# A fused two-attention kernel: the list that orders all of its work is replaced by another list

## The chip, the core and the metric

The kernel runs on one core of one Trainium2 chip. The core has five engines with queues of their own, filled when the program is built: TensorE (PE in the profile; its weight loads are shown as PEld), VectorE (DVE), ScalarE (ACT), GpSimd (POOL) and SyncE (SP). Every engine takes its instructions strictly in the order of its queue and waits, where needed, on semaphores of the others. The metric is the device time of one execution in microseconds (us); lower is better.

## The reference, cut to what matters

Two attentions over 2048 tokens of width 640 (32 heads of 20) are computed and laid side by side in a bf16 output of 2048 x 1280.

```python
# A: four segments of 512 tokens, with a memory carried from one to the next
for s in range(4):
    logits = einsum('bhqd,bhkd->bhqk', qs, ks) * scale + mask      # causal within the segment
    a_dot  = einsum('bhqk,bhkd->bhqd', softmax(logits), vs)
    pq     = phi(qs)                                               # phi(t) = t+1 if t>0 else exp(t)
    a_mem  = einsum('bhld,bhde->bhle', pq, M) / (einsum('bhld,bhd->bhl', pq, z) + 1e-6)
    o      = g * a_mem + (1 - g) * a_dot                           # g = sigmoid(beta)
    M      = M + einsum('bhld,bhle->bhde', phi(ks), vs);  z = z + phi(ks).sum(l)
out_A = o @ wo                                                     # q, k, v = x @ wq, wk, wv
# B: sliding window
mask   = (i - j >= 0) & (i - j < 256)
out_B  = (softmax(where(mask, q @ k.T * scale, -1e9)) @ v) @ wo    # q, k, v = x @ wqkv
```

## The kernel before

**Chunks and jobs.** The work is cut into eight chunks of 512 tokens, A and B in turn: chunk 0 is A's first segment, chunk 1 is B's first 512 tokens, up to chunk 7, B's last. Each chunk has generators ("jobs") that issue one piece of work at a time. Their names are letter, chunk, part: `k70` is the first part of the k projection of chunk 7. The letters are `q`, `k` and `v` (projections; `qk_job`, `v_job`), `d` (the update of A's memory), `o` (output projection, two halves of 320 columns for each of four tiles of 128 tokens; `final_job`) and `z0`, `z1` (the last two tiles of chunk 7, which are transposed on TensorE instead of by a DMA; `last_job`). A piece is one wide product of 128 rows, five of them to a tile of 320 or 512 columns.

**Score batches.** There are 153 batches of scores, `S` or `s` in the list (`score_batch`). A batch is a run of small products of 20 rows, `sc<-qA,kA` or `sc<-qB,kB` (L818), into two PSUM tiles; ScalarE then takes two exponentials of 128x1024 (L834) into `pt`. There are three PSUM score tiles of two banks (`NSC`) and ten `pt` (`NPT`). Masks are applied to `pt` by GpSimd (affine select, L873) or VectorE (L851).

**Value and memory products.** `A` in the list is the value product of one group of four heads (`av`, L887) or, in chunk 7, of one tile (`av_tile`, L908); `M` is the product with A's memory (`mem`, L934 or L939). VectorE turns the result (L953), then the row sum is inverted (L972, L978, L981) and GpSimd normalises (L991); where both a value and a memory product exist they are added by VectorE (L1004).

**Two banks.** Every wide product tile, value product and memory product accumulates in one of two PSUM banks (`m0`, `m1`). It can begin when the one before in that bank has been emptied: by the turn (L953) after `A` and `M`, by a cast (L557 for k and q, L734 and L739 for v, L1095 on VectorE or L1078 on ScalarE for o) after a projection tile.

**Forms.** Scores and value products use TensorE in tiles of 32 rows or columns. A wide product can be run whole (128x128 weights, L939) or as four products of 32 output columns (L934). The form is fixed per stretch between two score batches: where the list has `S` followed by an `A` before the next batch, the wide products of that stretch are issued in four; after `s` they are issued whole.

**Transfers.** q and k tiles are regrouped by a round trip to memory (L509, L517); so are the squares of v at the diagonals (L757, L783) and the feature maps of k (L651 out, L646 back, turned). The normalised `o` of a chunk goes out to `scr_o` (L1025) and comes back turned as `oT` or `xT` (DMA_TRANSPOSE, L1044), after which the `o` jobs can run. Weights come in by L319 and L331, x by L355. Most of these are in SyncE's queue.

**The order.** `body` builds the program with a model of the engines' clocks (class `Flow`). The string `PLAN` is the order of TensorE's work: the main loop pops its next entry and issues it as soon as its needs are met in that model, so TensorE's queue follows the list exactly. Instructions of the other engines (casts, masks, turns, norms, transfers) are put into their queues at the times that the model gives, so their order follows the list indirectly. `X*n` stands for n entries of X. "Slot n" is the stretch between batch n and batch n+1; batch 0 is the first.

## Time and profile before

| | |
|---|---|
| median of 3 runs | 330.41 us (329.88 to 330.71) |
| profiled execution | 330.69 us, of which 329.0 us is the span |
| granted TensorE clock | 1.00 |
| TensorE busy | 314.1 us (95%), 7180 matmuls |
| ScalarE busy | 299.8 us (91%), 334 instructions |
| GpSimd busy | 266.2 us (81%), 674 |
| VectorE busy | 257.7 us (78%), 534 |
| exponentials (L834) | 282.9 us, 306 of 1024 ns on average |
| masks on GpSimd (L873) | 178.7 us, 512 |
| turns (L953) | 61.3 us, 88 |
| score products (L818) | 39.9 + 33.4 us in the two largest groups |
| DMA | 47.12 MB in 75017 packets, mean 143 GB/s |

The span is the time from the first to the last instruction in the trace, the rest is around it. A row of a timeline is: start (us), duration, engine, line, operation, output <- inputs with sizes, how many instructions the row holds, and in brackets the idle time of the engine before it and what released it. In a row with several instructions the duration is that of the whole row. A row of the waits is: who waited, on what, the sum in us, how many times, and the longest.

### The profile page before, as it was taken

The page shows a single profiled execution, that of the slowest core. Times are in us where ns is not written, and L with a number is a line of the kernel's source. Part 1 is how long each engine was busy: PE and PEld are TensorE (multiplying, and loading weights), DVE is VectorE, ACT ScalarE, POOL GpSimd, SP SyncE. Part 2 cuts the span into 40 slices and gives each one's busy share as a digit, 9 for nine tenths or more (in the row PEclk, how much of TensorE's full clock was granted, in tenths as well). Part 3 has the DMA queues.
Part 4 walks back from the last instruction along what each step waited for, and adds up shares of the span by engine and source line. Part 5 has one row for each costly group of instructions (what it writes and reads, how often), then busy time and mean ns, then how long its engine had stood idle before and what let it go on. Part 6 is the DMA issues. An engine that isn't in the chain of part 4 may idle for free.

```text
span 329.0 us, 16969 instructions
## 1 busy us (share of the span) xinstructions
PE 314.1 (95%) x7180; PEld 177.2 (54%) x7215; DVE 257.7 (78%) x534; ACT 299.8 (91%) x334; POOL 266.2 (81%) x674
## 2 busy tenths in 40 slices
PE   8999999999999999999899999999999999999994
PEld 3454546555544455556554546456654445666662
DVE  6777757799877877999777897988777788976672
ACT  2979999999999998989899999899999999979972
POOL 8466689988769799977785999999975899989760
PEclk9999999999999999999999999999999999999999
DMA  7975846753679565265688146018758027398522
GB/s 206 400 249 142 186 140 115 162 168 70 166 190 190 106 166 166 44 137 148 126 223 176 30 86 181 20 36 171 143 175 179 14 53 183 110 234 164 115 95 67
DMA packets 75017, 47.12 MB, mean 143 GB/s; under 512 B 47133, under 2 KB 71933, under 8 KB 74941
## 3 DMA queue, kind: packets, MB, share of 16 engines
q1 hardware_dynamic: 74221, 45.38, 57.2%
q8 instruction: 56, 0.92, 1.1%
q10 hardware_dynamic: 720, 0.66, 0.7%
q14 instruction: 20, 0.16, 0.1%
HBM read 17.62 MB, written 16.79 MB: 105 GB/s over the span
## 4 chain that ended last, share of the span: by engine, by line
PE 48%; POOL 9%; ACT 7%; DVE 5%; issue 4%; POOLq 0%; ACTq 0%; DVEq 0%
PE m L939 25%; PE sc L818 10%; PE m L887 7%; ACT pt L834 6%; POOL pt L873 6%; PE m L934 5%; DVE tt L953 3%; POOL o L991 2%; PE m L908 1%; POOL u L991 1%; DVE pt L851 1%; PE m L686 0%; POOL rr L972 0%; ACT e L577 0%; POOL MZ L710 0%
## 5 line engine op out<-in xcount | busy, mean ns | idle before, releaser
L834 ACT ACTIVATE pt<-sc 128x1024 bf16<-128x1024 f32 (+2 forms) x306 | 282.9, 1024 | 14.0 <-PE sc L818 12.1
L873 POOL TENSOR_SCALAR_AFFINE_SELECT pt<-pt 128x128 bf16<-128x128 bf16 (+1 forms) x512 | 178.7, 377 | 47.9 <-ACT pt L834 40.4
L953 DVE STREAM_TRANSPOSE tt<-m 128x512 f32<-128x512 f32 x88 | 61.3, 709 | 24.7 <-PE m L887 16.8
L991 POOL TENSOR_TENSOR o<-tt,rr 128x320 bf16<-128x320 f32 x64 | 48.5, 759 | 3.6 <-DVE rr L981 2.6
L818 PE MATMUL sc<-qB,kB 20*64 20x64 bf16 (+2 forms) x1728 | 39.9, 217 | 0.8 <-ACT pt L834 0.5
L851 DVE TENSOR_TENSOR pt<-pt,ends 128x1024 bf16<-128x1024 bf16 (+2 forms) x50 | 36.5, 739 | 0.0
L939 PEld LDWEIGHTS <-xT 128*128 128x128 bf16 x286 | 25.8, 97 | 17.7 <-issue 6.8
L1095 DVE CAST ot<-m 128x320 bf16<-128x320 f32 x58 | 27.9, 486 | 8.3 <-PE m L939 7.0
L818 PEld LDWEIGHTS <-kB 20*64 20x64 bf16 (+1 forms) x1728 | 22.2, 98 | 22.6 <-issue 20.6
L818 PE MATMUL sc<-qA,kA 20*64 20x64 bf16 (+4 forms) x1024 | 33.4, 237 | 0.5 <-ACT pt L834 0.3
L939 PEld LDWEIGHTS <-oT 128*128 128x128 bf16 x244 | 21.6, 97 | 11.3 <-issue 1.6
L818 PEld LDWEIGHTS <-kA 20*128 20x128 bf16 (+1 forms) x1024 | 13.6, 97 | 22.8 <-issue 21.8
L939 PE MATMUL m<-wBv,xT 128*128 128x320 bf16 x147 | 24.2, 299 | 1.0 <-DVE tt L953 0.4
L887 PE MATMUL m<-pt,vA 128*32 128x192 bf16 (+3 forms) x512 | 23.6, 274 | 0.2
L939 PE MATMUL m<-xT,wBq 128*128 128x512 bf16 x73 | 20.6, 380 | 0.9 <-DVE tt L953 0.3
L939 PE MATMUL m<-wo_A,oT 128*128 128x320 bf16 x125 | 20.4, 300 | 0.3 <-DVE kA L557 0.3
L939 PE MATMUL m<-wv_A,xT 128*128 128x320 bf16 x119 | 20.0, 300 | 0.6 <-DVE qA L557 0.5
L939 PE MATMUL m<-xT,wBk 128*128 128x512 bf16 x70 | 19.6, 380 | 0.7 <-issue 0.3
L739 DVE CAST vB<-m 128x320 bf16<-128x320 f32 x32 | 15.6, 486 | 4.7 <-PE m L939 2.4
L557 DVE CAST kB<-m 128x512 bf16<-128x512 f32 x20 | 13.6, 680 | 6.7 <-PE m L939 5.7
L557 DVE CAST qB<-m 128x512 bf16<-128x512 f32 x20 | 13.8, 688 | 6.5 <-PE m L934 3.2
L939 PE MATMUL m<-wo_B,oT 128*128 128x320 bf16 x109 | 18.7, 300 | 0.2 <-DVE ot L1095 0.2
(127 smaller groups left out, 468.8 us busy)
## 6 DMA issues: line engine op xcount, KB each, us to landing
out_dram<-ot SPq DMA_DIRECT2D x29, 160.0 KB
scr_o<-o SPq DMA_DIRECT2D x28, 160.0 KB
xT<-in_B_x_dram SPq DMA_DIRECT2D x8, 288.0 KB
xT<-in_A_x_dram SPq DMA_DIRECT2D x8, 256.0 KB
scr_pk<-e SPq DMA_DIRECT2D x15, 128.0 KB
vS<-vA SPq DMA_DIRECT2D x16, 87.0 KB
vL<-vB SPq DMA_DIRECT2D x8, 174.0 KB
scr_kA<-kA SPq DMA_DIRECT2D x16, 60.0 KB
```

What stands on the lines that cost most here:

```text
L557: nc.vector.tensor_copy(out=dst[:, m, at:at + L], in_=ps[:, :])
L739: nc.vector.tensor_copy(out=dst, in_=src)
L818: nc.tensor.matmul(ps[j // 2][h0:h1, j % 2, c0:c0 + nq], lhsT=k[rows, g, k0:k0 + h1 - h0], rhs=q[rows, g, q0:q0 + nq], start=True, stop=Tr ...
L834: nc.scalar.activation(out=pt[:, :, lo:hi], in_=ps[i][:, :, lo:hi], func=ACT.Exp, scale=self.scale)
L851: nc.vector.tensor_tensor(out=blk, in0=blk, in1=self.ends[:, c0, :].unsqueeze(1).unsqueeze(1) .to_broadcast([P, 2, n // SH, SH]), op=ALU.mult)
L873: nc.gpsimd.affine_select(out=blk, in_=blk, pattern=pat, compare_op=ALU.is_ge, fill=self.zero, base=base, channel_multiplier=mul)
L887: nc.tensor.matmul(O[HD * j:HD * j + HD, q0:q0 + nq], lhsT=v[:, at:at + HD], rhs=pts[j // 2][:, j % 2, c0:c0 + nq], start=(n_ == 0), stop= ...
L934: self.nc.tensor.matmul(ps[s, 0:n], lhsT=lhsT[:, s], rhs=rhs, start=start, stop=stop, tile_position=(0, HD * j), skip_group_check=True)
L939: self.nc.tensor.matmul(ps[:, 0:n], lhsT=lhsT, rhs=rhs, start=start, stop=stop, skip_group_check=True)
L953: self.nc.vector.transpose(out=tt[:], in_=O[:, :])
L991: nc.gpsimd.tensor_tensor(out=to[:] if add_to else to, in0=a, in1=b, op=ALU.mult)
L1095: nc.vector.tensor_copy(out=ot[:, 320 * hf:320 * hf + 320], in_=ps[:, 0:320])
```

## The change

Only the string `PLAN` differs. Both lists hold every entry the same number of times, apart from the two letters of the score batches: `S` goes from 77 to 83 and `s` from 76 to 70. 114 of the 154 stretches (before the first batch, between batches, after the last) hold other work than before. The jobs, the buffers, the model and the transfers themselves are the same code.

```diff
-    "k00*5 q00*5 k01*4 S k01 q01*5 S v00*16 S v00*4 k02 S k02*4 k03*5 q02*3 S q02*2 q03*5 k04*5 "
-    "A S A q04*5 v01 s v01*9 s k10*5 S v01*10 S q10*2 A S q10*3 q11*3 S q11*2 q12*5 A s k11*5 "
-    "k12*2 S k12 A k12*2 S v10*9 S v10*10 S v10 A k13*2 s k13*3 q13*4 S q13 A s k14*5 q14*2 S "
-    "q14*2 A q14 S d2*5 v11*4 S v11*8 S v11*3 A v11 S v11*4 d2*2 S q20*4 A s q20*5 s q20*6 "
-    "k20*6 S k20*4 A s k20*5 v20*5 S v20*3 A v20 s v20 q23*5 v20 s v20*8 S v20 q23*5 A s v21*5 "
-    "k23*3 S k23*2 A s o00*5 k23*5 v21*5 S o00*5 v21*5 S A v21*5 s q30*5 k30*2 S k30*3 A s "
-    "k30*6 S k30*4 q30 S q30*4 A s M q30*5 v30*2 s v30*3 A S M v30*10 s A M s v30*5 q33*4 S q33 "
-    "A s M k33*5 q33 s q33*4 k33*3 S k33*2 A s M v31*8 S v31*2 A M S v31*10 S A M S d4*5 q40*3 "
-    "S q40*2 d4*2 A s M k40*5 s q40*10 S v40*5 k40*5 A S k40*5 v40*5 S v40*2 A v40*2 S v40*6 "
-    "q43*3 S q43*7 S k43*10 A S o00*5 A s o10*10 s o00*5 o10*5 S o00*10 v41*4 S v41 o10*5 A "
-    "o00*2 s o00*3 v41*5 S A o00*5 s v41*8 s v41*2 o10*7 S o10*3 A o10*3 s o10*2 q50*5 S A "
-    "k50*3 s k50*2 k53*5 s q50*5 k50*2 s k50*3 A S k50*2 M k50*3 s A M S v50*5 q50*5 s A M S "
-    "v50*10 S v50*5 A s M q53*6 s q53*4 k53*2 S k53*3 A S M v51*9 S v51 A M S v51*10 S A M S "
-    "q60*5 d6*5 s d6*2 A S k60*2 M k60*3 q60*5 s k60*6 S k60*4 q60*5 A S q63*5 v60*5 S A v60*5 "
-    "s q63*5 v60*2 S v60*3 k63*5 S v60*5 A k63 S k63*4 o10*5 S o20*3 A s o20*7 s v61*10 S v61*5 "
-    "A v61*5 S o30*5 o20*5 S o20*5 A o20 S o20*4 o30*4 s o30 o20*10 S A o20*4 S o20 k70*7 S k70 "
-    "A k70*2 S k70*5 v70*3 S v70*2 q70*4 s q70 A M s q70*5 s A q70*5 s v70*5 k73*2 s k73*3 A s "
-    "M v70*9 s v70 A M s q73*2 M q73*3 s k73*5 q73*2 s q73*3 A s o30*5 M s v71*5 A s M v71*5 "
-    "o30*4 s o30 A M s v71*8 s v71*2 A M s o30*9 s o30 o40*5 o30*5 s o30*5 A s o40*10 s o40*15 "
-    "A s o40*5 o50*5 s o40*5 o50*5 s A o50*4 s o50*6 s A o50*4 s o50*8 s o50*8 s A o60*5 s "
-    "o60*10 o70*5 s A o70*3 s o70*2 o60*7 s o60*8 o71*2 s o71*3 o60*2 A o60*3 z0 o71*5 o60 A "
-    "o60 z0 o60*3 z0 z1*2 z0 z1*2 ")
+    "k00*5 q00*5 k01*4 S k01 q01*5 v00*2 s v00*14 S v00*4 k02*5 S q02*5 q03*3 S q03*2 k03*5 "
+    "k04*5 A S A q04*5 v01 S v01*9 s v01*5 k10 S k10*4 v01*5 S q10*2 A S q10*3 q11*3 S q11*2 "
+    "k11*5 A S q12*5 k12*2 S k12 A k12*2 S v10*7 s v10*12 S v10 A k13*2 s k13*3 k14*4 S k14 A S "
+    "q13*5 q14*2 S q14 A q14*2 s d2*5 v11*2 S v11*10 S v11*3 A v11 S v11*4 d2*2 S k20 A k20*3 S "
+    "k20 q20*4 s q20*11 k20 S k20*4 A s k20*5 v20*5 S v20*4 A s v20 q23*6 s q23*4 v20*4 S v20 "
+    "v21*5 A S v20*5 k23*3 S A k23*2 S o00*5 k23*5 v21*4 S v21 o00*5 v21*6 S v21*4 A s q30*5 "
+    "k30*2 S k30*3 A S q30*6 S q30*4 k30*2 S k30*3 A S M v30*5 k30*2 s A k30*3 s M q33*5 v30 s "
+    "v30*4 A s M v30*8 S A v30*2 s k33*2 M k33*3 S v31*5 q33*2 S q33*3 A S k33*2 M k33*3 v31*3 "
+    "S v31*2 A M s v31*10 S A M s d4*5 q40*3 S q40*2 d4*2 A S M k40*5 q40*3 S q40*7 S v40*5 "
+    "k40*5 A S k40*5 v40*5 S v40 A v40*3 S v40*6 q43*3 S q43*7 S k43*10 A S o10*5 A s o10*5 "
+    "o00*5 s o00*10 o10*5 S v41*5 o00*4 S o00 v41*5 A v41 S v41*4 o00*5 S A o00*5 S o10*5 v41*5 "
+    "s o10*9 S o10 A o10*3 S o10*2 k53*5 S A k50*4 s k50*6 s q50*7 s q50*3 A S k50*2 M k50*3 S "
+    "A M s v50*5 q50*5 s A M s v50*10 S v50*5 A S M q53*6 S q53*4 k53*2 S k53*3 A S M v51*10 s "
+    "A M s v51*9 S v51 A M s d6*5 q60*5 S d6*2 A S k60 M k60*6 S k60*3 q60*5 S q60*5 k60*5 A S "
+    "q63*5 v60*5 S A v60*4 S v60 q63*5 k63*3 s k63*2 o10*5 S v60*5 A v60*2 s v60*3 k63*5 S "
+    "o20*3 A S o20*2 v61*6 s v61*4 o20*5 o30 S o30*4 A v61*5 s o30*5 v61*5 S o20*5 A S o20*9 s "
+    "o20*9 S o20*2 A o20*4 s o20 k70*5 S A v70*5 s q70*5 k70 S k70*4 q70*2 s q70*3 A s q70*2 M "
+    "q70*3 s k70*5 A s v70*5 k73*2 s k73*3 A s M v70*10 s A M s q73*2 M q73*3 s q73*5 k73 s "
+    "k73*4 A s o40*5 M s o30*5 A s M o40*5 o30*3 s o30*2 A M s v71*5 o30*3 s o30*2 A M s o30*5 "
+    "v71*4 s v71*10 s v71 A o30*4 s o30 o40*5 o30*2 s o30*3 o40*15 A s o40*9 s o40 o50*7 s "
+    "o50*3 A o50 s o50*9 s A o50*2 s o50*9 s o50*9 s A o60*5 s o70*5 o60*5 s o60*5 A o60*3 s "
+    "o60*2 o70*5 o71*2 s o71*3 o60*5 s o60*5 A o60*5 z0 o71*5 A z0 o60*2 z0 o60*3 z1*2 z0 z1*2 ")
```

Some places in the lists, slot by slot:

| slot | before | after |
|---|---|---|
| 36, 37, 38 | `o00*5 k23*5 v21*5`, `o00*5 v21*5`, `A v21*5` | `o00*5 k23*5 v21*4`, `v21 o00*5 v21*6`, `v21*4 A` |
| 59, 60 | `M k40*5`, `q40*10` | `M k40*5 q40*3`, `q40*7` |
| 129, 130, 131 | `o30*5 M`, `v71*5 A`, `M v71*5 o30*4` | `o40*5 M`, `o30*5 A`, `M o40*5 o30*3` |
| 134, 135, 136 | `v71*2 A M`, `o30*9`, `o30 o40*5 o30*5` | `o30*2 A M`, `o30*5 v71*4`, `v71*10` |
| 137, 138, 139 | `o30*5 A`, `o40*10`, `o40*15 A` | `v71 A o30*4`, `o30 o40*5 o30*2`, `o30*3 o40*15 A` |
| 148, 149 | `o60*10 o70*5`, `A o70*3` | `o70*5 o60*5`, `o60*5 A o60*3` |
| 150, 151 | `o70*2 o60*7`, `o60*8 o71*2` | `o60*2 o70*5 o71*2`, `o71*3 o60*5` |

## The prediction

> **What bounds the kernel now.** I read the page first (busy shares, the chain that ended last), then the waits, then the busy time by stretches, then timelines at single places. "Slot n" is the work the list puts between score batch n and score batch n+1 (153 batches, 0 to 152).
>
> ```profile
> span 329.0 us, 16969 instructions
> PE 314.1 (95%) x7180; PEld 177.2 (54%) x7215; DVE 257.7 (78%) x534; ACT 299.8 (91%) x334; POOL 266.2 (81%) x674
> q8 instruction: 56, 0.92, 1.1%
> PE 48%; POOL 9%; ACT 7%; DVE 5%; issue 4%; POOLq 0%; ACTq 0%; DVEq 0%
> ```
>
> ```profile
> POOL pt L873 <- ACT pt L834: 40.4, 57, 2.1
> ACT pt L834 <- PE sc L818: 12.1, 22, 1.8
> PE m L939 <- DVE tt L953: 1.3, 6, 0.3
> PE m L887 <- issue: 0.8, 1, 0.8
> PE sc L818 <- ACT pt L834: 0.8, 4, 0.3
> ```
>
> ```profile
> core 0: us, PE busy (x) PEld busy (x) DVE busy (x) ACT busy (x) POOL busy (x), PEclk, DMA share, GB/s
> 8.20:46.30 38.10, 37.32 (x713) 19.24 (x717) 27.81 (x59) 35.38 (x42) 23.75 (x70) 1.00 0.75 221
> 46.30:79.50 33.20, 32.24 (x796) 18.28 (x785) 26.80 (x54) 32.35 (x39) 31.14 (x71) 1.00 0.60 146
> 187.50:219.70 32.20, 31.15 (x723) 16.95 (x716) 27.88 (x57) 29.80 (x33) 31.12 (x74) 1.00 0.32 76
> 255.00:299.70 44.70, 43.85 (x997) 25.14 (x997) 36.80 (x79) 42.67 (x46) 40.70 (x106) 1.00 0.52 118
> ```
>
> TensorE (PE) is busy 95% of the span and ScalarE (ACT) 91%; in every stretch of the middle both are within a few per cent of full, at the granted clock of 1.00. Neither alone is the bound: ScalarE has run dry 22 times waiting for scores (12.1 us in all), and TensorE has waited for score buffers that the exponentials had not freed (0.8 us by this view, which sees only the part beyond modelled ends). So the end is set by a path that changes sides: it runs along TensorE up to a place where ScalarE ran dry, and along ScalarE up to a place where TensorE waited for it. An order can win in two ways: score batches placed so that ScalarE stays fed, and fewer waits in the stretches where TensorE carries the path.
>
> **TensorE's own work.** The order listing of the two built programs counts 192 groups of four 32-column matmuls for the wide products before and 193 after (360+408 and 396+376 instructions), 881 and 880 whole matmuls, 340 and 339 changes between array shapes; every score, value and memory product is there as often as before.
>
> ```profile
> 236.41 0.86 PE L934 MATMUL m<-wo_A,oT 128*32 128x320 bf16 x20
> 237.10 0.28 PE L887 MATMUL m<-pt,vX 128*32 128x256 bf16 x4
> ...
> 309.27 0.84 PE L939 MATMUL m<-wo_B,xT 128*128 128x320 bf16 x5
> 310.05 0.40 PE L818 MATMUL sc<-qB,kB 20*128 20x128 bf16 x16
> ```
>
> Five products of 320 columns take 0.69 us in four-column form up to a value product of the same shape (236.41 to 237.10), and 0.78 us whole up to a score, where the array shape changes (309.27 to 310.05): 0.136 a piece either way and 0.1 for the change. One change fewer is 0.1 us; the exchange of forms is nothing, and there is no cover to lose, since this is TensorE's own time. **Term 1: -0.1** (ends -0.1 and 0).
>
> **Where the score batches stand.** I laid the lists side by side and priced each slot by such spacings. 114 of 154 stretches hold other work, but the distance of a batch from the start of the list changes by at most 0.9 us (batch 3) and stands 0.2 us earlier at batch 152. Both lists are variants of one layout. What counts is the places where ScalarE had run dry.
>
> ```profile
> 130.34 1.02 ACT L834 ACTIVATE pt<-sc 128x1024 bf16<-128x1024 f32 x1 [0.66 <-PE sc L818]
> 293.20 3.79 ACT L834 ACTIVATE pt<-sc 128x1024 bf16<-128x1024 f32 x4 [1.78 <-PE sc L818]
> 310.56 7.48 ACT L834 ACTIVATE pt<-sc 128x1024 bf16<-128x1024 f32 x8 [0.44 <-PE sc L818]
> ```
>
> Slot 59 gains three pieces of q40 and slot 60 loses them: batch 60 comes 0.65 later, batch 61 at its old place. ScalarE, which needs 2.04 for a batch (7.48 for eight exponentials shows the rate), then finishes batch 60 0.1 after the moment at which it now starts batch 61: +0.1. Slots 140 to 148 put batch 149 0.68 earlier, so its wait of 0.44 goes; but slot 149 grows from 1.61 to 2.38 us of TensorE work, batch 150 stands 0.09 later in the list than before, and about 0.05 of the gain is left at the last exponential. The long wait before batch 140 (1.78) grows with slot 139 (eighteen products of 320 where there were fifteen) while slots 135 to 138 give as much back. The others move by 0.1 to 0.4, up and down, and return within some slots. **Term 2: 0** (ends -0.6, the 0.44 and 0.1 to 0.2 more kept, and +0.4, the largest lateness that a dry place gets, if it stays).
>
> **Waits for the two accumulator banks.** Every wide product, value product and memory product takes one of two banks and waits for VectorE (DVE) to empty the one before it.
>
> ```profile
> 259.87 0.59 PE L887 MATMUL m<-pt,vA 128*32 128x448 bf16 x12
> ...
> 260.54 0.48 PE L818 MATMUL sc<-qA,kA 20*128 20x448 bf16 x8
> 260.95 0.39 PE L939 MATMUL m<-pq,MZ 128*128 128x512 bf16 x1
> 261.48 1.38 PE L939 MATMUL m<-wBv,xT 128*128 128x320 bf16 x9
> ```
>
> Here a value product, a score batch and one memory product (M) are followed by a product that needs the value product's bank: 0.53 us from M to the next start where 0.216 is M's spacing, so 0.31 lost, with 0.68 us of other work since the value product's last piece. Where 0.68 covers, 0.16 to 0.39 are lost in this trace; at 0.78 about 0.2; from 0.89 on next to nothing. After a value or output tile (a shorter evacuation) a cover of 0.81 loses about 0.07. Counting covers in both lists: below 0.8 us after a value or memory product 19 before, 15 after; output and v tiles at 0.81 and under 26 before, 32 after; two q/k tiles come down to 0.86 and 1.04 us where some 1.17 is wanted. Priced alike, the sum of what is lacking is 9.4 before and 9.5 us after, and of that the part in the stretches where TensorE carries the path grows by 0.24. **Term 3: +0.25** (ends -0.5, if only the four removed shortest covers count, and +0.6, if all new ones do).
>
> ```profile
> 82.97 0.34 PE L818 MATMUL sc<-qB,kB 20*128 20x256 bf16 x8
> 83.60 0.84 PE L939 MATMUL m<-wo_A,oT 128*128 128x320 bf16 x5 [0.29 <-DVE kA L557]
> 84.61 0.84 PE L939 MATMUL m<-wv_A,xT 128*128 128x320 bf16 x5 [0.17 <-DVE vA L734]
> ```
>
> ```profile
> 82.50 0.45 DVE L598 TENSOR_TENSOR e<-r,e 128x512 bf16<-128x512 bf16 x1
> 82.87 0.68 DVE L557 CAST kA<-m 128x512 bf16<-128x512 f32 x1
> 83.47 0.68 DVE L851 TENSOR_TENSOR pt<-pt,ends 128x1024 bf16<-128x1024 bf16 x1
> 84.07 0.48 DVE L734 TENSOR_TENSOR vA<-m,omg 128x320 bf16<-128x320 f32 x1
> ```
>
> Slot 37 is of another kind: there the cover is long enough, but VectorE is behind. The k tile's cast stands behind the feature map of an earlier k tile (0.42 + 0.45), and the v tile's behind a mask of 0.68. Batch 37 takes 0.33 to the next start elsewhere, so the output product starts 0.3 late, and the v product another 0.33 late (84.61 less 83.60 less 0.68). In the new order the cast stands ahead of that feature map, between the two masks, and the output product comes one piece later. This stretch feeds a place where ScalarE ran dry. I take two thirds of the 0.65 as gone: **term 4: -0.45** (ends -0.65 and 0). What is late next is the fourth v tile, which now begins ahead of batch 38.
>
> **Code loading.** In slot 73 the weight loads stop in the middle of a value product, and nothing the profile shows ended the stop:
>
> ```profile
> 159.25 0.10 PEld L887 LDWEIGHTS <-vL 128*32 128x32 bf16 x3
> 160.30 0.09 PEld L887 LDWEIGHTS <-vL 128*32 128x32 bf16 x1 [0.95 <-issue]
> ```
>
> The instruction queue moved 0.92 MB in 56 pieces, one for each 256 or so of TensorE's instructions, and this stop is the only one near 1 us. The new list has the same number of instructions ahead of slot 73 and 3.51 us of work for the 256 before the stop (3.48 before). **Term 5: 0** (ends -0.95, the stop gone, and +0.95, a second one). The Trainium skill, Runtime: NRT & Kernel Launch, section Instruction fetch mechanics, says that the sequencer streams blocks of 256 instructions ahead and that this is hidden by the slower issue; the 0.95 us speak against it at this place, and by the rule alone the stop would be no matter of the order and the sum would keep the same terms without it.
>
> **Loads and queues.** SyncE's queue is emptied in order. In the new list the last chunk's transposed tiles are wanted earlier:
>
> ```profile
> 286.44 2.58 SPq L1044 DMA_TRANSPOSE oT<-scr_o  x1
> 302.46 1.22 SPq L1044 DMA_TRANSPOSE xT<-scr_o  x1
> 310.09 1.21 SPq L1044 DMA_TRANSPOSE xT<-scr_o  x1
> ```
>
> The first product of tile 1 (o71) moves from slot 151 into slot 150 behind seven products. Batch 150 stands some 1.6 us behind batch 149 (310.05), takes 0.65, and seven products 0.95: 313.3, 2.0 us after the issue at 310.09 has ended. The first use of tile 0 before was at 309.27, 5.6 us after its issue ended (302.46 + 1.22), and does not wait; it moves to the front of slot 148, 1.4 us earlier. The transpose at 286.44 waits for a buffer that o30 frees; o30 ends in slot 139 instead of 137, some 2.6 us later, and scr_o6 and all behind it on SyncE start later by what the queue's pauses do not absorb. Loads of the last output weights, on the other hand, leave SyncE before the last regrouping instead of within it, and o10, o30 and o40 begin earlier in slots where their tiles have long been stored. **Term 6: 0** (ends 0 and +1.9: the 5.6 are the only proven landing, and 3.7 of them may be needed where 2.0 are left, rounded up for the queue). GpSimd and VectorE keep their counts (674 and 534); ScalarE's list moves by three feature-map steps.
>
> **The tail** from the last exponential on has the same steps in both lists; the last value product stands 0.14 us later on TensorE, behind masks that were just ready, and what TensorE last waits for is the last normalised tile (o):
>
> ```profile
> 321.90 0.40 PE L1118 MATMUL sc<-one,o 128*128 128x128 bf16 x4 [0.33 <-POOL o L991]
> ```
>
> **Term 7: 0** (ends 0 and +0.14).
>
> **Sum.** -0.1 + 0 + 0.25 - 0.45 + 0 + 0 + 0 = -0.3 us. The profiled execution took 330.69 us (329.0 of span and 1.7 around it), 0.28 above the median 330.41 of the runs: 330.4 against its own time, 330.1 against the median. I give 330.3. About 0.3% (1 us) is what a measurement of this kernel can tell from no change.
>
> **Rivals.** *Late transposed tiles (slower).* If o71 and o70 wait for SyncE, the wait stands right ahead of the last two score batches and goes through to the end: term 6 at its upper end, 330.3 + 1.9 = 332.2. It decides when tile 1 needs over 2.0 us from the end of its issue to use, or when the queue is 0.5 to 1 us later than now. For it: three things now hang on o30's end. Against it: the pauses in SyncE's queue. Chance 0.15. *Bank waits at the new places (slower).* More covers at 0.81 and the VectorE order at new places cost like slot 37 cost before: two such places at 0.65 on top of the sum, 331.6. Chance 0.17. *The stop goes (faster).* The block that came late in slot 73 comes in time: 330.3 - 0.95 = 329.35. For it: the stop came once in 56 blocks. Against: equal counts ahead of it. Chance 0.14. *ScalarE stays fed (faster).* Terms 2 and 3 at their lower ends: 330.3 - 0.6 - 0.75 = 328.95. Chance 0.18. *The order does nothing to speak of* is the forecast itself: 0.36, from 329.5 to 331.3.
>
> The range reaches from a little below the last faster case to a little above the slower one: 328.5 to 332.6. Faster by over 0.3%: 0.14 + 0.18 = 0.32; within: 0.36; slower: 0.15 + 0.17 = 0.32.
>
> **What would show it.** Right: TensorE busy within 0.5 us of 314.1; ScalarE's waits for scores still between 11 and 13 us; no wait of kA or vA casts in slot 37; the stop of about 0.95 in slot 73 again; no product of L939 waiting for a DMA after 300 us. Wrong: a second stop without a releaser, a product waiting for xT or oT, or waits for scores that change by over 1 us in the last 50 us.

## The result and the profile after

The kernel with the new list takes 333.91 us (333.64 to 336.02), the one before 330.47 us in the same comparison. The ratio is 1.0121 with a 95% interval of 1.0078 to 1.0164: slower by 1.2%, beyond the upper end of the range that was given (332.6). The profiled execution took 333.64 us with a span of 331.9. An execution that took over 1.5% longer than the fastest of the same kernel is left out of the medians and ratios below; there are two such (335.16 and 342.15 us).

The page of the profile after, its lines on the span, the engines and the chain that ended last:

```profile
span 331.9 us, 16976 instructions
PE 314.8 (95%) x7182; PEld 176.5 (53%) x7218; DVE 258.0 (78%) x534; ACT 300.3 (90%) x334; POOL 265.6 (80%) x674
...
PE 45%; POOL 12%; DVE 10%; ACT 4%; issue 3%; DMA 3%; SPq 1%; POOLq 0%; ACTq 0%; DVEq 0%
```

The engines do as much as before; the loss is in waiting. The chain has a new entry, DMA with 3%, and VectorE's part doubled from 5% to 10%. The waits of the profile after (who waited for what, sum in us, how often, longest) name transfers for which TensorE waited; the profile before has no wait of TensorE for xT or oT out of scr_o:

```profile
ACT pt L834 <- PE sc L818: 12.4, 24, 1.9
...
PE m L939 <- DVE tt L953: 1.6, 7, 0.3
...
PEld L939 <- DMA xT<-scr_o: 1.2, 1, 1.2
...
PEld L939 <- DMA oT<-scr_o: 0.7, 1, 0.7
...
PE m L887 <- DVE vB L739: 0.7, 1, 0.7
```

Where the time was lost is read from the exponentials: the start of a batch's first exponential in the trace after, less the same in the trace before.

| batch | 49 | 54 | 73 | 74 | 100 | 121 | 144 | 145 | 149 | 150 | 151 |
|---|---|---|---|---|---|---|---|---|---|---|---|
| after less before, us | 0.0 | 2.0 | 2.0 | 1.0 | 1.0 | 0.7 | 0.7 | 1.4 | 1.4 | 2.2 | 3.1 |

Two places lose (batches 50 to 54, and from batch 145 on), one gains (slot 73). ScalarE's timeline at the first place before, and after at the two places, with idle times in brackets:

```profile
103.06 22.37 ACT L834 ACTIVATE pt<-sc 128x1024 bf16<-128x1024 f32 x24
```

```profile
109.25 5.61 ACT L834 ACTIVATE pt<-sc 128x1024 bf16<-128x1024 f32 x6 [0.61 <-PE sc L818]
115.34 1.94 ACT L834 ACTIVATE pt<-sc 128x1024 bf16<-128x1024 f32 x2 [0.49 <-PE sc L818]
118.10 7.45 ACT L834 ACTIVATE pt<-sc 128x1024 bf16<-128x1024 f32 x8 [0.82 <-POOL rr L972]
...
304.04 5.61 ACT L834 ACTIVATE pt<-sc 128x1024 bf16<-128x1024 f32 x6 [0.56 <-PE sc L818]
310.15 3.77 ACT L834 ACTIVATE pt<-sc 128x1024 bf16<-128x1024 f32 x4 [0.51 <-POOL pt L873]
314.62 1.94 ACT L834 ACTIVATE pt<-sc 128x1024 bf16<-128x1024 f32 x2 [0.69 <-PE sc L818]
317.36 3.77 ACT L834 ACTIVATE pt<-sc 128x1024 bf16<-128x1024 f32 x4 [0.80 <-PE sc L818]
```

Before, ScalarE went through batches 47 to 58 without a pause (the 24 exponentials of the first row). Three things stand ahead of the pauses after. The first is on VectorE (TensorE's rows below it):

```profile
111.26 0.68 DVE L851 TENSOR_TENSOR pt<-pt,ends 128x1024 bf16<-128x1024 bf16 x1
113.42 0.49 DVE L739 CAST vB<-m 128x320 bf16<-128x320 f32 x1 [1.48 <-PE m L934]
113.83 0.68 DVE L851 TENSOR_TENSOR pt<-pt,ends 128x1024 bf16<-128x1024 bf16 x1
```

```profile
110.88 0.85 PE L939 MATMUL m<-wBv,xT 128*128 128x320 bf16 x5
111.57 0.59 PE L939 MATMUL m<-xT,wBq 128*128 128x512 bf16 x2
...
112.48 0.83 PE L934 MATMUL m<-xT,wBq 128*32 128x512 bf16 x12
```

The cast of v31's first tile (`vB`) waits 1.48 us. The product that it empties is the first of these rows and had ended near 111.7; the L934 that the cast's row names is a product of q, which the cast does not read and which ended just before it. The second is in SyncE's queue and what waits for it (SyncE's second transpose before, which the prediction does not show, then SyncE after, then TensorE after):

```profile
297.36 3.81 SPq L1044 DMA_TRANSPOSE oT<-scr_o  x1
```

```profile
290.58 2.76 SPq L1044 DMA_TRANSPOSE oT<-scr_o  x1
...
302.90 2.50 SPq L1044 DMA_TRANSPOSE oT<-scr_o  x1
305.58 1.86 SPq L1044 DMA_TRANSPOSE xT<-scr_o  x1
...
312.03 1.21 SPq L1044 DMA_TRANSPOSE xT<-scr_o  x1
```

```profile
113.97 0.59 PE L887 MATMUL m<-pt,vA 128*32 128x448 bf16 x12 [0.66 <-DVE vB L739]
...
308.85 0.85 PE L939 MATMUL m<-wo_A,oT 128*128 128x320 bf16 x5 [0.61 <-DMA oT<-scr_o]
...
316.46 0.45 PE L939 MATMUL m<-wo_B,xT 128*128 128x320 bf16 x2 [0.84 <-DMA xT<-scr_o]
```

The four transposes are issued 4.1, 5.5, 3.1 and 1.9 us later than before, and o60 (slot 147) and o71 (slot 150) wait for theirs; measured from start to start, TensorE loses 0.68 and 1.00 us. The third is the loading of code. TensorE's weight loads after, at two of the stops:

```profile
108.99 0.11 PEld L818 LDWEIGHTS <-kA 20*64 20x64 bf16 x4 [0.68 <-issue]
...
303.43 0.45 PEld L818 LDWEIGHTS <-kB 20*64 20x64 bf16 x46 [0.66 <-issue]
```

Counted in TensorE's queue, these stops lie where a block of 256 instructions ends (every 256 from the 194th on, waits on semaphores counted), as does the one of slot 73 before. After, there are four: 0.79 us in slot 50, 0.48 in slot 69, 0.32 in slot 98 and 0.74 in slot 145, measured from start to start beyond the usual spacing. The one in slot 73 is gone.

### The profile page after: what moved, and what is told of

It is laid out like the page before. It is cut to its first block, busy times and chain, and to the rows that moved or that the text cites. A ratio compares the mean times of both kernels' runs of the same rounds, so it can differ in the third digit from the quotient of the medians.

```text
span 331.9 us, 16976 instructions
## 1 busy us (share of the span) xinstructions
PE 314.8 (95%) x7182; PEld 176.5 (53%) x7218; DVE 258.0 (78%) x534; ACT 300.3 (90%) x334; POOL 265.6 (80%) x674
## 4 chain that ended last, share of the span: by engine, by line
PE 45%; POOL 12%; DVE 10%; ACT 4%; issue 3%; DMA 3%; SPq 1%; POOLq 0%; ACTq 0%; DVEq 0%
PE m L939 22%; PE sc L818 9%; POOL pt L873 7%; PE m L887 7%; PE m L934 5%; ACT pt L834 4%; DVE tt L953 4%; POOL o L991 2%; DVE pt L851 1%; DMA xT<-scr_o 1%; DMA vU<-vB 1%; PE m L908 1%; POOL u L991 1%; DVE ot L1095 1%; DVE vA L734 1%
## 5 line engine op out<-in xcount | busy, mean ns | idle before, releaser
L834 ACT ACTIVATE pt<-sc 128x1024 bf16<-128x1024 f32 (+2 forms) x306 | 282.9, 1022 | 15.7 <-PE sc L818 12.4
L953 DVE STREAM_TRANSPOSE tt<-m 128x512 f32<-128x512 f32 x88 | 61.6, 710 | 22.3 <-PE m L887 13.8
L1095 DVE CAST ot<-m 128x320 bf16<-128x320 f32 x58 | 28.1, 487 | 12.4 <-PE m L939 10.1
L818 PE MATMUL sc<-qA,kA 20*64 20x64 bf16 (+4 forms) x1024 | 34.1, 237 | 1.2 <-issue 0.6
L939 PEld LDWEIGHTS <-xT 128*128 128x128 bf16 x274 | 24.8, 97 | 17.4 <-issue 5.6
L939 PE MATMUL m<-wBv,xT 128*128 128x320 bf16 x140 | 23.0, 299 | 1.1 <-DVE tt L953 0.6
L939 PE MATMUL m<-wo_A,oT 128*128 128x320 bf16 x130 | 21.9, 300 | 0.8 <-DMA oT<-scr_o 0.6
L939 PE MATMUL m<-xT,wBq 128*128 128x512 bf16 x79 | 21.9, 381 | 0.7 <-issue 0.2
L939 PE MATMUL m<-xT,wq_A 128*128 128x512 bf16 x79 | 21.0, 380 | 0.5
L939 PE MATMUL m<-xT,wBk 128*128 128x512 bf16 x66 | 18.7, 380 | 0.6 <-issue 0.3
L991 POOL TENSOR_TENSOR u<-tt,rr 128x320 bf16<-128x320 f32 x24 | 17.4, 726 | 1.3 <-DVE rr L978 1.1
```

What stands on the lines that cost most here:

```text
L818: nc.tensor.matmul(ps[j // 2][h0:h1, j % 2, c0:c0 + nq], lhsT=k[rows, g, k0:k0 + h1 - h0], rhs=q[rows, g, q0:q0 + nq], start=True, stop=Tr ...
L834: nc.scalar.activation(out=pt[:, :, lo:hi], in_=ps[i][:, :, lo:hi], func=ACT.Exp, scale=self.scale)
L939: self.nc.tensor.matmul(ps[:, 0:n], lhsT=lhsT, rhs=rhs, start=start, stop=stop, skip_group_check=True)
L953: self.nc.vector.transpose(out=tt[:], in_=O[:, :])
L991: nc.gpsimd.tensor_tensor(out=to[:] if add_to else to, in0=a, in1=b, op=ALU.mult)
L1095: nc.vector.tensor_copy(out=ot[:, 320 * hf:320 * hf + 320], in_=ps[:, 0:320])
```

## The experiments

In the diffs, OLD and NEW are the two lists, and "NEW[50..53]" means slots 50 to 53 of the new one; at these slots both lists have issued the same work, so that they can be joined. Ratios are against the kernel before, with 95% intervals.

**The two halves.**

```diff
-PLAN = OLD
+PLAN = NEW[..128] + OLD[129..]     # the first
+PLAN = OLD[..128] + NEW[129..]     # the second
```

> The new list up to slot 128, the old one from slot 129 on. Theory (two losses that add up, 2.0 us in slots 50 to 53 less 1.0 in slot 73, and 2.2 us from slot 129 on): 330.4 + 0.9 = 331.3. Rival (the loss of slots 50 to 53 is absorbed later, the end alone costs): 330.4; rival (the end is late whatever its list, pushed by the start): 333.9.

Measured: 332.44 us, 1.0049 (1.0032 to 1.0066), 1.8 us over the kernel before in the same comparison (330.64), twice the 0.9 of the theory.

> The old list up to slot 128, the new one from slot 129 on. Theory (the new list's end is late by its own: stop in slot 145, wait for oT in slot 147, wait for xT in slot 150): it loses what the new list loses from batch 129 to 152, 3.08 - 0.91 = 2.2 us: 332.6. Without the stop in slot 145 (the border falls 6 instructions later in the same score batch) 331.9. Rival (the end is late because of what came before): 330.5.

Measured: 333.42 us, 1.0107 (1.0068 to 1.0145), 2.8 us over the kernel before. Both halves lose by themselves; neither pushes the other. Their losses, 1.8 and 2.8, add up to more than the 3.4 of the whole list, and they do not share all of its stops. The end costs more than the trace of the new list let expect. In the second kernel's trace three waits follow each other in it:

```profile
307.20 0.29 PE L908 MATMUL m<-pt,vB 128*32 128x128 bf16 x6 [0.61 <-POOL pt L873]
...
308.11 0.85 PE L939 MATMUL m<-wo_A,oT 128*128 128x320 bf16 x5 [0.39 <-DMA oT<-scr_o]
...
316.27 0.45 PE L939 MATMUL m<-wo_B,xT 128*128 128x320 bf16 x2 [1.14 <-DVE pt L851]
```

The first lies at a block border (0.79 us by start to start), the others are the two transposes (0.50 and 1.31); the last names VectorE, but it is the same product that waited for xT in the new list, and the row of its weight load names xT (1.47 us). The late block does not add to the wait for oT: o60 starts 3.4 to 3.9 us after the issue of its transpose has ended in four traces, with no late block ahead of it (the new list, 3.45), and with one of 0.79 (here, 3.60), 0.76 (NEW[129..147], below, 3.86) and 0.29 us (the kernel of "Undoing the two moves", below, 3.40).

**Slots 50 to 53.** One kernel undoes them, one has them (with 46 to 49, without which they can't be joined to the old list with v30 ending in slot 49) and nothing else.

```diff
+PLAN = NEW[..49] + OLD[50..53] + NEW[54..128] + OLD[129..]
+PLAN = OLD[..45] + NEW[46..53] + OLD[54..]
```

> The new list up to slot 128 with slots 50 to 53 from the old one, and the old one from slot 129 on: beside the kernel that has the new list up to 128 (332.44 us), only the four slots 50 to 53 are undone. There the first tile of v31 is projected in slot 51 instead of 53, and its cast stood 1.2 to 1.5 us at the head of VectorE's queue until a transfer that reads the same tile (vU<-vB) had landed. Theory (that wait holds up the value product behind it and goes through to the end): 332.44 - 1.0 to 1.4 = 331.2, and no wait of VectorE for that transfer. Rival (ScalarE's path absorbs it by slot 100): 332.4.

Measured: 331.10 us, 1.0008 (0.9992 to 1.0025), 0.2 us over the kernel before (330.89); VectorE has no such wait.

> The old list with slots 46 to 53 alone from the new one (v30 ends in slot 49 instead of 48, the first tile of v31 in slot 51 instead of 53). Theory (the cast of v31 behind the transfer that reads its tile): VectorE waits 1.2 to 1.5 us for vU<-vB near 112 us, batches 53 and 54 come 0.5 and 1.0 to 1.4 later, and it stays: 330.6 + 1.2 = 331.8. Rival (absorbed, or owed to the slots ahead of it): 330.6.

Measured: 332.16 us, 1.0043 (1.0026 to 1.0060), and the wait of the cast is in its trace:

```profile
112.27 0.49 DVE L739 CAST vB<-m 128x320 bf16<-128x320 f32 x1 [1.48 <-PE m L934]
```

VectorE's timeline in the kernel with the new list up to slot 128:

```profile
110.95 0.68 DVE L851 TENSOR_TENSOR pt<-pt,ends 128x1024 bf16<-128x1024 bf16 x1
112.86 0.49 DVE L739 CAST vB<-m 128x320 bf16<-128x320 f32 x1 [1.24 <-DMA vU<-vB]
```

Here the releaser is named: the transfer vU<-vB. When v30, the other half of the same tile `vB`, is complete, three transfers read it (`v_ends`, L783; issued at 108.5 to 110.4 in the trace after). The new list projects v31 two slots earlier, and its cast writes the tile that they still read, so it waits until they have landed; VectorE takes its queue in order, so the masks, the reciprocal and the cast of q stand behind it, and the value product of slot 52 waits for the bank. Undoing these four slots gives back 1.6 us (1.8 over the kernel before, then 0.2), and slots 46 to 53 alone cost 1.3 (330.89 to 332.16). A late block in slot 50, the rival at this place, is not needed: between batches 52 and 54 ScalarE falls behind the kernel before by 1.58 us in the new list (block late by 0.79), by 1.34 in the list up to slot 128 (0.28) and by 1.56 in the list with slots 46 to 53 alone, where no block is late there; with the four slots undone it is 0.00. In what is left of the first half the intervals tell no loss. The 1.3 us of slots 46 to 53 alone are not this wait by itself: that list has 12 more TensorE instructions, so all later borders move, and in its trace the stop of slot 73 is gone (1.0 gained) and two blocks near 233 and 242 us are late (0.60 and 0.90).

**The end: late queue or early use.**

```diff
+PLAN = OLD[..128] + NEW[129..139] + OLD[140..]
+PLAN = OLD[..139] + NEW[140..]
+PLAN = OLD[..128] + NEW[129..147] + OLD[148..]
```

> The old list with slots 129 to 139 alone from the new one (v71 ends in slot 137, o30 in slot 139); slots 140 to 152 are old, so that o60 starts in slot 147 and o71 in slot 151 as before. Theory A (SyncE's queue is late because v71 and o30 end later; the late transposes cost what the new list loses): the transposes for o60 and for the last two tiles are issued 2 to 5.5 us later than before, o60 waits 0.5 to 0.7 us, tile 1 less than 1: 330.6 + 0.7 = 331.3, and 332.2 if o71 waits too. Theory B (it is the earlier use in slots 148 to 150): 330.6.

Measured: 332.00 us, 1.0038 (1.0019 to 1.0057). The profiled execution (333.43 us) was the slowest of its twelve, and o60 does not wait for its tile in it; o50 waits for the transpose before, in slot 140, and a late block stops TensorE just ahead of o60:

```profile
293.75 0.85 PE L939 MATMUL m<-wo_B,oT 128*128 128x320 bf16 x5 [0.47 <-DMA oT<-scr_o]
...
307.60 0.29 PE L908 MATMUL m<-pt,vB 128*32 128x128 bf16 x6 [1.39 <-POOL pt L873]
```

The transposes are issued 1.2 to 3.2 us late here, not 2 to 5.5. How the 1.1 us of the median divide between late transposes and that block, this one trace cannot tell.

> The old list with slots 140 to 152 alone from the new one (o70 at the head of slot 148, o71 in slot 150), the queue of SyncE ahead of them as before. Theory A (late queue): tile 1 is transposed at about 310 us as before and o71 wants it at 313.3; landed 4.3 us after its issue (312.03 to 316.4 in the new list's trace) it would still be 1.0 late, no more: 330.6 to 331.6. Theory B (early use): 330.6 + 1.0 to 1.3 = 331.7 with a wait for xT in slot 150 of 1.0 or over, and no wait for oT in slot 147.

Measured: 331.36 us, 1.0006 (0.9985 to 1.0027), and no wait for xT or oT in its trace: with the old slots ahead, the second xT was issued at 308.46, earlier than before (310.09):

```profile
308.46 2.43 SPq L1044 DMA_TRANSPOSE xT<-scr_o  x1
```

> The old list with slots 129 to 147 from the new one; slots 148 to 152, with o71 in slot 151, stay old. Beside the kernel with slots 129 to 152 from the new list (333.4 us). Theory (the wait of o71 for the transposed last tile but one, 1.0 to 1.3 us, takes both: the late queue and the use in slot 150): it goes, 333.4 - 1.2 = 332.2, with the wait of o60 in slot 147 left. Rival (the late queue is enough): 333.4 and a wait for xT in slot 151.

Measured: 331.75 us, 1.0027 (1.0003 to 1.0050), 1.0 us over the kernel before (330.74). Its trace has the wait of o60 and none of o71, although the transpose for o71 is issued as late as in the new list:

```profile
312.16 1.21 SPq L1044 DMA_TRANSPOSE xT<-scr_o  x1
```

```profile
307.82 0.85 PE L939 MATMUL m<-wo_A,oT 128*128 128x320 bf16 x5 [0.36 <-DMA oT<-scr_o]
```

So a wait for oT comes with the late queue alone, and the wait for xT needs both the late queue and the use in slot 150: slots 129 to 139 alone cost 1.1 us, slots 140 to 152 alone nothing that the interval tells from zero, and both together 2.8.

**Undoing the two moves in the new list.**

```diff
+PLAN = NEW[..49] + OLD[50..53] + NEW[54..147] + OLD[148..]
```

> The new list with nine slots undone: 50 to 53 (the first tile of v31 back in slot 53) and 148 to 152 (o71 back in slot 151). Theory (the loss is a few waits at these places): 333.9 - 1.3 - 1.2 = 331.4. Rival (the loss is spread over the new order, its late queue above all): 333 or more.

Measured: 332.21 us, 1.0041 (1.0014 to 1.0067), 1.5 us over the kernel before (330.74), where the new list was 3.4 over it. So the nine slots hold about 2.0 of the 3.4 us, not the 2.5 of the theory. Of the rest, o60 still waits 0.73 us for oT, and the list with slots 129 to 147 alone lost 1.0; the last 0.5 is within what the intervals leave open.

**Block borders.** Some wide warm-up products at the start are replaced by small ones; all borders move, and nothing else does.

```diff
-        f.pe = max(f.pe, 1500.0)
+        f.pe, skip = max(f.pe, 1500.0), 1                 # 4 in the third kernel
         while f.pe + 700.0 < max(self.done[(0, "x", 0)], self.done[("wk_A", 0)]):
-            self.wide(ps, ones(P), ones(L), L, True, True)
-            f.flush()
+            f.on_pe("full", mm_ns(L), L) if skip > 0 else self.wide(ps, ones(P), ones(L), L, True, True); skip -= 1; f.flush()
+        # 35 in the third kernel
+        for _ in range(7): self.nc.tensor.matmul(ps[0:HD, 0:HD], lhsT=ones(HD), rhs=ones(HD), ...)
```

> The old list, with one of the wide warm-up products at the start replaced by seven of 32x32, so that TensorE has 12 more instructions ahead of the first projection; all else is the same. Theory (the 256-instruction blocks of code arrive late where a block is used up fast): each block border moves 12 instructions towards the start of the program, the border in slot 73 leaves the value product, its stop of 0.95 us goes: 329.4 us. Rival (the stop belongs to that value product, wherever the border lies): 330.4 us and a stop of about 0.95 in slot 73 again.

Measured: 330.52 us, 0.9998 (0.9979 to 1.0017). The stop in slot 73 is gone, as the theory has it, and the time is the same: the trace has two others at borders, 0.82 us at 249.5 and 0.49 at 292.2.

> The new list with the same 12 more instructions at the start. Theory (late blocks are part of the loss): the stops of 0.79 us in slot 50, 0.48 in slot 69, 0.32 in slot 98 and 0.74 in slot 145, which all lie at a block border in the new list's trace, go or shrink; of them 0.5 us (slot 50) lies on the path for certain and slot 145 may be absorbed by the waits for transposed tiles behind it: 333.4 us with 0.5 gained, 332.6 with both. Rival (these stops are of the work, not of the border): 333.9.

Measured: 336.31 us, 1.0154 (1.0131 to 1.0178). A miss in the sum: the stops of slots 50, 69 and 145 are gone, but others came at or just behind borders (0.76 us at 38.1, 0.89 at 251.8, and 0.72 at 206.1, the border that had stopped TensorE for 0.32 in slot 98), and TensorE, earlier by the stop of slot 145, waited longer for the same transposes:

```profile
310.07 0.85 PE L939 MATMUL m<-wo_A,oT 128*128 128x320 bf16 x5 [1.05 <-DMA oT<-scr_o]
...
312.31 1.51 PE L939 MATMUL m<-wo_B,xT 128*128 128x320 bf16 x5 [1.05 <-DMA xT<-scr_o]
```

The last row takes 1.51 us where five such products took 0.85. The busy time by stretches of the same kernel shows why: the granted clock (third number from the end) fell.

```profile
308.00:312.00 4.00, 2.21 (x97) 1.38 (x85) 1.87 (x5) 3.09 (x4) 3.23 (x9) 1.00 0.75 172
312.00:316.00 4.00, 3.69 (x29) 1.99 (x30) 0.99 (x2) 1.49 (x3) 2.00 (x5) 0.57 0.56 150
316.00:320.00 4.00, 4.00 (x160) 2.68 (x158) 2.42 (x6) 3.27 (x4) 2.27 (x5) 1.00 0.16 49
```

At 0.57 for 4 us some 1.7 us are lost on top of the waits.

> The old list with 62 more instructions of TensorE at the start (four wide warm-up products replaced by 35 of 32x32). Theory (a block of code is ready about 2.35 us after its fetch starts, and the fetch starts 0.8 to 1.5 us after the border before, later when the transfer engines are full; a block that is used up sooner makes TensorE stop): by the old list's trace five blocks would then be used up within 1.9 to 2.4 us (borders near 147, 162, 171, 239 and 248 us), each a stop of 1.1 to 1.7 us, of which ScalarE's queue of scores covers some: 333 to 337 us. Rival (where the borders lie does not matter): 330.7.

Measured: 334.70 us (332.99 to 335.97), 1.0120 (1.0081 to 1.0159). Three of the five named borders stop TensorE by over 0.3 us (0.78 near 163, 0.36 near 173, 1.13 near 241), and others that were not named do too. Weight loads in this trace:

```profile
26.10 0.15 PEld L818 LDWEIGHTS <-kA 20*64 20x64 bf16 x14 [1.12 <-issue]
...
164.34 0.39 PEld L939 LDWEIGHTS <-xT 128*128 128x128 bf16 x4 [0.95 <-issue]
...
241.79 0.10 PEld L818 LDWEIGHTS <-kB 20*64 20x64 bf16 x2 [1.04 <-issue]
```

The same order of the same work, with the borders at other places, costs 4.0 us (330.74 to 334.70). Where the borders lie matters.

**What makes a block late.** In ten traces (before, after, the two halves, the two kernels of slots 50 to 53, NEW[129..139] and NEW[140..] alone, and both lists with borders moved by 12) the packets of the instruction queue are set beside TensorE's program. No block is used less than 2.18 us after its packet starts, and in 25 of 30 stops it is used 2.2 to 2.6 us after. The packet starts some time after the border before; grouped by the busy share of the transfer engines between that border and the packet (a stop is the time across the border beyond what the same instructions take elsewhere; 39 packets that start ahead of the border by these traces are left out):

| share of the transfer engines | blocks | mean delay of the packet, us | longest | stops over 0.25 us |
|---|---|---|---|---|
| under 0.3 | 86 | 0.75 | 1.64 | 0 |
| 0.3 to 0.6 | 66 | 1.07 | 2.53 | 0 |
| 0.6 to 0.8 | 155 | 1.21 | 2.86 | 11 |
| 0.8 to 1.0 | 114 | 1.55 | 2.67 | 8 |
| over 1.0 | 90 | 1.49 | 3.28 | 11 |

That is side by side, not cause. The stop of slot 73 recurs with the old list, so traffic was taken away there, in `phi_q` (one or two of chunk 4's four stores of pq left) and in the output stores.

```diff
-            for j in range(4):
+            for j in range(1 if n == 4 else 4):
...
-            self.store_out(ot, out2d[r:r + P, col:col + self.D], slot, t, on)
+            self.store_out(ot, out2d[r:r + P, col:col + (64 if n in (0, 1) else self.D)], slot, t, on)
```

> The old list; the stores of the output tiles of chunks 0 and 1 (o00, o10: slots 67 to 77 and one more later) write 64 of their 640 columns, so those output rows are left incomplete; nothing else changes, TensorE's instructions are the same one by one. Theory (the code block that slot 73 needs is fetched late because these stores fill the transfer engines): its fetch, 2.2 to 2.4 us after the border before it in five traces with this list, starts 0.8 to 1.4 us after it, the stop of 0.4 to 1.0 us in slot 73 goes, 330.7 - 0.7 = 330.0. Rival (the fetch is late for another reason, as by TensorE's own instructions): the stop stays at 0.4 to 1.0 us, 330.7.

> The same cut of the stores of chunks 2 and 3 (o20, o30: from slot 107 on), none of which is near slot 73. Both accounts: the stop of 0.4 to 1.0 us in slot 73 stays. If it goes here too, the cut stores act in another way than by the traffic at that place.

Measured: 330.62 us, 1.0001 (0.9974 to 1.0028), with the stop still there, and 330.63 us, 1.0009 (0.9986 to 1.0032), with no stop there in its trace although nothing was changed at that place. So the output stores are not what does it (the share stayed 0.67), and one trace alone proves little: the same program stops at a border in one execution and not in the next.

> The old list; of the four stores of pq that chunk 4 sends out at 154.6 to 156.2 us, one is left (the other three quarters are read back from what chunk 2 had stored, so part of A's third segment takes the wrong queries into its memory product). In the old list's trace the packets of these stores were most of the traffic between the border before slot 73 and the late fetch. TensorE's instructions are the same. Theory (traffic makes the fetch of the code block late): the fetch, 1.8 to 2.4 us after the border in six of seven traces with this border, starts at most 1.3 us after it, and the stop of 0.4 to 1.0 us in slot 73 goes: 330.0. Rival (the fetch is late for another reason): 1.8 to 2.4 us and a stop again, 330.6.

> Two of the four stores of pq in chunk 4 are left (the other half read back from chunk 2's). Theory: the fetch lies between, about 1.3 to 2.0 us after the border, a stop of under 0.4 us or none in slot 73. Rival: 1.8 to 2.4 us and a stop of 0.4 to 1.0.

> The same, and the output stores of chunks 0 and 1 cut to 64 columns besides (those rows incomplete): the least traffic of the three at that place. Theory: fetch at most 1.2 us after the border, no stop in slot 73. Rival: as with all stores.

Measured: 330.27 us, 1.0002 (0.9979 to 1.0025); 330.39 us, 1.0004 (0.9984 to 1.0024); 330.27 us, 0.9984 (0.9959 to 1.0009). The packet for slot 73, by what is left of the traffic (packets and stops as above):

```
stores left near slot 73              share  packet after border, us     stop, us
all (5 traces: before and 4 others)   0.66 to 0.69   1.85 to 2.42        0.52 to 1.04
small output stores (chunks 0, 1)     0.67   2.03                        0.52
all (1 trace, stores cut elsewhere)   0.61   1.13                        none
two of four pq                        0.70   1.99                        0.49
one of four pq                        0.33   1.12                        0.46
one of four pq, small output stores   0.52   0.89                        none
```

The stretch between the border and the fetch in the old list and in the kernel with the least traffic (busy time by stretches; second number from the end is the share of the transfer engines):

```profile
155.50:157.90 2.40, 2.38 (x82) 1.75 (x80) 1.83 (x4) 2.40 (x4) 2.14 (x6) 1.00 0.72 109
```

```profile
155.50:157.90 2.40, 2.40 (x74) 1.41 (x66) 1.89 (x5) 2.40 (x5) 1.75 (x4) 1.00 0.32 58
```

With less traffic the packet starts about 1 us earlier (in the kernel with the least the share is 0.52 over the 0.89 us up to its packet, and 0.32 over the same 2.40 us as before). With one store of four it started early and TensorE stopped all the same, because that packet took 1.49 us where others took 0.9. Two stores taken away did not lower the share, and changed nothing. So traffic is one cause of late blocks at this place, as far as one trace of each can say; the one early packet among the traces with all of it shows that it is not the only one, and what else decides stays open. In time, a stop gone here is at most the 0.5 us of the last kernel, which its interval does not tell from zero.

**A faster list from the parts.** The first half of the new list gained a little at three places.

```diff
+PLAN = OLD[..40] + NEW[41..45] + OLD[46..96] + NEW[97..99] + OLD[100..114] + NEW[115..121] + OLD[122..]
```

> The old list with three stretches from the new one, in which the trace of the new list's first 129 slots gained on the old one: slots 41 to 45 (0.33 us by batch 45), 97 to 99 (0.5 by batch 100) and 115 to 121 (0.4 by batch 120). Theory (these gains are lasting and add up): 330.7 - 1.2 = 329.5. Rival (they are swings of a path that changes sides, and are given back some slots later): 330.7.

Measured: 330.72 us, 1.0002 (0.9979 to 1.0024). The gains were swings: in its trace the 0.35 us gained by batch 45 and the 1.3 gained by batch 99 are given back by batches 51 and 100. No list that was tried beats the kernel before.

## Why the prediction was wrong

It gave 330.3 us with a range up to 332.6; 333.9 was measured. Its steps, one by one:

- **Term 1, TensorE's own work (-0.1).** TensorE was busy 314.8 us, 0.7 more than before, a little outside the 0.5 that was named as right. The program has three matmuls more (the page counts two, since a few records are missing from a trace), which cannot make that. Where the 0.7 comes from is not shown. It is not what decided.
- **Term 2, dry places (0).** Right: batch 60 came 0.65 later and batch 61 at its old place; the 0.1 that was added for slot 59 rests on a misread rate, since eight exponentials in 7.48 us, two to a batch, are 1.87 a batch and not 2.04; the wait before batch 140 grew from 1.78 to 1.87; the wait of 0.44 before batch 149 went, and the gain was lost again in slots 149 to 151. But the sum of ScalarE's waits for scores, 12.4 us and so within the 11 to 13 named, says nothing of the loss.
- **Term 3, bank waits (+0.25).** The waits for the turn (L953) grew from 1.3 to 1.6 us, which is the size that was given. The count of covers could not see the bank wait that cost most, since there the cover was long enough and the cast itself was held up by a transfer.
- **Term 4, slot 37 (-0.45).** Wrong by its size: batch 36 came 0.7 us earlier, and batch 38 0.14 later. Of the two waits one went (for kA), the other (for vA) stayed with 0.33, and the dry place behind took what was left: ScalarE waited 0.40 us before batch 38, as before (0.43). Gain: none.
- **Term 5, code loading (0).** The stop in slot 73 went, worth 1.0 us, and four others came, of which those in slots 50 and 145 held up ScalarE by 0.6 each. Both ends of the term came true at once. The step that failed is its ground: equal counts of instructions and equal work ahead of slot 73. The counts were not equal: the new list has six fewer TensorE instructions ahead of batch 73 (6486, before 6492), so the border falls six later in the same value product. In the runs, what decides is the time between two borders against the start of the packet plus 2.2 us or more (up to 3.0 at the stops), at each border and not at one; and the packet's start varies by over 2 us. The page Runtime: NRT & Kernel Launch of the Trainium skill (section Instruction fetch mechanics), cited there, has the fetch hidden by the slower issue; 30 stops of 0.27 to 1.61 us in ten traces speak against it here.
- **Term 6, loads and queues (0, ends 0 and 1.9).** This is the step that failed most. Its mechanism was right, and it was priced at its lower end. The list moves v71's end by three slots and o30's by two; the first transpose was then issued 4.1 us later, where the prediction had o30's end 2.6 us later and let the queue's pauses absorb part of it, and the second 5.5 us later. o71 needed its tile 3.2 us after the end of the issue (313.24 to 316.46) where 2.0 were left; the 3.7 by which the upper end was set stand in no row, and what the runs show where a tile is waited for is 2.8 to 3.2 for o71 and 3.4 to 3.9 for o60. The wait of o60 in slot 147, 0.68 us, was not on the list of uses at all. Together 1.7 us in the trace, and 2.8 for this stretch in the run that has it alone, with the block that is late there.
- **Term 7, the tail (0).** The last exponential ends 3.08 us later and the span 2.9: nothing more was lost behind it.
- **What no term had.** The cast of v31 behind the transfer that reads its tile: 1.3 to 1.6 us. The prediction looked for late casts in VectorE's own order and for late tiles that TensorE reads; it did not ask which transfer still reads a tile that a moved step writes.

Of the rivals, the first (late transposed tiles, 332.2) named the larger loss, and the second (waits at new places through VectorE's order, 331.6) the kind of the other. They were priced one at a time; both happened, which gives 330.3 + 1.9 + 1.3 = 333.5. That this comes near the 333.9 is in part luck: the 0.45 of term 4 did not come, one stop went (1.0) and four came, and none of that is in the sum.

## What to carry to other kernels

When a list moves a step, follow each tile in both directions: when what it reads has landed, and which transfers still read what it writes; a cast that meets such a transfer stops everything behind it in its engine's queue. A transfer that is ready just in time has no slack left, so a later queue and an earlier use must be priced together, not each against the old slack. A kernel near its floor has stops of TensorE at block borders of its program that any change of the order deals anew, 0.3 to 1.6 us each here, and not the same in two executions of one program (the stop of slot 73 lay between 0.5 and 1.0 us in six traces with near the same traffic, and was missing in a seventh): differences of that size between two orders are no verdict on the orders.

## What was not expected

In two of the traces the granted clock fell near the end, each time after TensorE had stood still for much of a few us. In the new list with moved borders TensorE was busy for 2.21 of the 4 us from 308 to 312, in which the two waits of 1.05 us lie, so it stood still for 1.8; the mean clock of the next 4 us was 0.57. In the list with slots 129 to 139 new, a late block near 306 us stands ahead of the same; the busy time by stretches of that kernel:

```profile
306.00:308.00 2.00, 0.61 (x48) 0.46 (x36) 0.00 (x0) 2.00 (x3) 1.79 (x5) 1.00 1.05 150
308.00:312.00 4.00, 4.00 (x43) 2.11 (x32) 1.86 (x4) 1.93 (x3) 2.30 (x5) 0.57 0.39 116
```

Here TensorE stood still for 1.4 of the 2 us ahead (2.00 less 0.61). A mean of 0.57 over 4 us means half the clock for 3.4 us (0.43 x 4 / 0.5). Where TensorE stood still for 1.14 us within 3 (the old list with slots 129 to 152 new), the clock stayed at 1.00. So a stop can cost more than its own length: the one of 1.6 us near 306 was followed by 3.1 us lost between batches 147 and 149. How much standstill in what stretch is needed, two cases do not tell. The Trainium skill, TensorE: Matmul & The Clock Gate (Part 1: The HAM clock gate), says that the clock goes to half after an idle window of about 3.4 us. The half rate agrees with these rows, while a wholly idle window of that length was not needed: 1.4 us of standstill in the one case and 1.8 in the other stand ahead of the fall.

One of the four executions of the new list took 336.02 us at a mean granted clock of 0.992, the other three 333.6 to 334.0 at 0.998 or more. Whether the clock fell in it at such a place is not shown.
